# One more dependency on the transposes of the second expert: they are held until both tiles of a pair are normalised

## The chip, the cores and the metric

The kernel runs on one core of a Trainium2 chip. The metric is the time of one execution on the device in microseconds (us); the kernel before takes 1237.52 us, the median of three runs. TensorE is written PE (its weight loads, which overlap with matmuls, PEld), VectorE DVE, ScalarE ACT, GpSimd POOL, and SyncE, which issues the transfers, SP.

## What is computed

An attention without softmax is followed by two expert layers. The change lies in the second expert alone:

```python
h = x @ w_in                                   # 4608 x 512 times 512 x 1024
h_max = np.max(h, axis=-1, keepdims=True)
e = np.exp(h - h_max)
sm = e / (np.sum(e, axis=-1, keepdims=True) + 1e-09)
solu = h * sm
mu = np.mean(solu, axis=-1, keepdims=True)
var = np.mean((solu - mu) ** 2, axis=-1, keepdims=True)
ln = (solu - mu) / np.sqrt(var + 1e-06) * g_ln
return (ln @ w_out).astype(np.float32)         # times 1024 x 512
```

## The kernel before

The 4608 tokens are 36 tiles of 128, and the second expert takes them two at a time: 18 pairs, numbered 0 to 17, each with a tile 0 and a tile 1. Every product is one level of Strassen (seven block products in place of eight), and every block product is made in three passes (`mm3`, lines 191 to 196): high part times high part on L192, high times the low part of the right side on L193, and the low part of the left side times high on L194. So a matmul's line tells which pass it is, not which product.

A pair goes through three functions.

- `second(u)` makes h: seven products of two steps with three passes each, 42 matmuls with 512 columns. Their names in the trace are `ps<-rxa,rwi` and `ps<-rxb,rwi`. DVE and ACT empty the banks (L1135, L1142, L1149), which gives two tiles of 128 x 1024 for the softmax and the normalisation (`soft`); the last step of that, a `tensor_scalar` on DVE (L1188), ends for one tile after the other.
- `second_out(u)`, first half: 16 transposes on PE (L1200), four for each half q of each tile n, every four into one bank of PSUM. They are four tasks, added in the order (1,0), (1,1), (0,0), (0,1) as (tile, half). Then come the Strassen sums: ACT copies block (1,0) (L1212), DVE makes four sums (L1209: S1 from (1,1), S3 and S2 from (0,0), S4 from (0,1)). Each of the seven left sides is split into a high part by ACT (L1226) and a low part, called its correction below (L1227). The blocks A11 = (0,0), A12 = (0,1) and A22 = (1,1) are corrected by DVE, the four sums by POOL, and in the last pair two of the sums by DVE as well.
- `second_out(u)`, second half: seven products in the order A11, S2, S1, A12, S3, S4, A22, of 12 matmuls with 256 columns each (84 in all), named `ps<-rg,rwo`, `ps<-e2r,e2r` and `ps<-ws,e2r`. DVE (L1248) and ACT (L1252) empty the banks, and SP sends the rows out (L1274).

The four transpose banks and the three banks of the seven products come from one ring of four banks; for the last two pairs the transposes take theirs from the ring that `second` uses.

The order on each engine is not written by hand. Every piece of work is a task with an engine, a planned duration, the keys that it reads and writes, and a wished time `at`; `Flow.run` plays the tasks through once while the kernel is built, and whenever an engine is free in that play it takes, among the tasks that can start, the one with the smallest `at`, and among equals the one that was added first. The instructions are issued in that order. On the chip each engine keeps to it and waits where a result is not there yet. The wished times of the work around the change are: transposes and sums of pair u 17.03 us after the pair's start, `second` of the next pair 20.75 us after it, and the products of the second half 28.08 us after it.

Of the kernel before, what the change touches and what calls it, by code (L numbers as in the profile page):

```python
# [79 lines left out]
class Flow:  # L80
# [36 lines left out]
    def add(self, eng, dur, fn, r=(), w=(), at=0.0, ps=False):  # L117
        t = Task()
        t.eng, t.dur, t.fn, t.at = eng, dur, fn, at
        t.port = eng in ("POOL", "DVE") and not ps  # L120
        t.deps, t.next, t.end, t.left, t.seq = set(), [], None, 0, len(self.tasks)
        for k in {*r, *(self.pool_of[k] for k in (*r, *w) if k in self.pool_of)}:
            if k in self.writer:
                t.deps.add(self.writer[k])
            self.readers.setdefault(k, []).append(t)
        for k in w:
            t.deps.update(self.readers.get(k, ()))
            if k in self.writer:
                t.deps.add(self.writer[k])
            self.writer[k], self.readers[k] = t, []  # L130
        t.deps.discard(t)
        self.tasks.append(t)
# [48 lines left out]
def tile_kernel(ctx, tc, qkv, tail, g2, w1, w2, gl, out):  # L181
    nc = tc.nc
    PE, ACT, DVE, POOL, SP = nc.tensor, nc.scalar, nc.vector, nc.gpsimd, nc.sync
    flow = Flow()
    add = flow.add
# [930 lines left out]
    def h_name(u):  # L1116

        return "h3" if u == NU - 1 else "h2"
# [73 lines left out]
    def second_out(u, at, early=0.0):  # L1192

        bks, banks = {}, hbank if u >= NU - 2 else accs
        for n, q in ((1, 0), (1, 1), (0, 0), (0, 1)):
            bk = bks[n, q] = banks()

            def turn(n=n, q=q, bk=bk):
                for c in range(4):
                    PE.transpose(buf[bk][:, c * P:(c + 1) * P], buf[h_name(u), n][:, (4 * q + c) * P:(4 * q + c + 1) * P],  # L1200
                                 buf["ident"])

            add("PE", 0.44, turn, r=[(h_name(u), n), "ident"], w=[bk], at=at)

        def a(n, q):
            return buf[bks[n, q]].rearrange("p (c t) -> p c t", t=P)
# [10 lines left out]
        for o in (A11, S2, S1, A12, S3, S4, A22):  # L1217
# [3 lines left out]
            else:  # L1221
# [7 lines left out]
                r=[*keys, ("xth", o)], w=[("xtl", o)], at=at, ps=o in (A11, A12, A22))  # L1229
# [42 lines left out]
        for n in range(2):  # L1272
            t, k = 2 * u + n, rows[n]
            add("SP", 0.73, lambda t=t, k=k: SP.dma_start(out=out[t * P:(t + 1) * P, :], in_=buf[k]),  # L1274
                r=[k, ("out half", k, 0), ("out half", k, 1)], w=[("out", t)], at=at)
# [42 lines left out]
    def t_step(i):  # L1318
        return T0 + STEP_A * i
# [5 lines left out]
    for i, (n, c) in enumerate(order):  # L1325
        at = t_step(c + 2 * n) - CV_AHEAD
# [115 lines left out]
    for i in range(NSTEP):  # L1442
        m, c = divmod(i, CPP)
        at, d = t_step(i), STEP_A
# [31 lines left out]
    at = T1_  # L1476
# [17 lines left out]
    for n, item in enumerate([*items, None]):  # L1494
        at = item["at"] if item else T_E2
# [16 lines left out]
        else:  # L1512
# [6 lines left out]
            for b in (B11, T2, T1, B21, T3, B22, T4):  # L1519
                for kk in range(2):  # L1520
                    for part in range(2):
# [3 lines left out]
                            r=[("bd", kk, 0, b), ("bd", kk, 1, b)] + ([("b", b)] if part or kk else []), w=[("b", b)],  # L1525
                            at=at)
# [34 lines left out]
    for i in range(2 * NOP):  # L1561
        o, part = divmod(i, 2)
        if i < 8:
# [3 lines left out]
            r=[("lwd", c, o) for c in range(NC // 2)], w=[("lw", o, part)], at=T_E2 + i)  # L1567
    for u in range(NU):
        at = T_E2 + E2_AT + PAIR_C * u
        last = u == NU - 1  # L1570
        if u:
            prep_second(u, at - E2_LEAD - (LAST_PREP if last else 0))
        if last:
            rooms = [(n, i) for n in ("sf", "xf") for i in range(2)]
            flow.change(lambda: None, (*rooms, *((("xf", i), n) for i in range(2) for n in range(2))),
                        [(n, i) for n in ("h3", "e3") for i in range(2)])
            for i in range(2):
                buf["h3", i], buf["e3", i] = (buf[n, i].rearrange("p a b -> p (a b)") for n in ("sf", "xf"))
        second(u, at - (LAST_LEAD if last else 0))
        if u < NU - 2:  # L1580
            second_out(u, at + TR_LAG)
        elif last:

            second_out(u - 1, at - PAIR_C + TR_LAG - LAST_TR, LAST_TR)
            second_out(u, at - LAST_LEAD + TR_LAG - LAST_TR1, LAST_TR1)
# [51 lines left out]
```

## Time and profile before

| | |
|---|---|
| three runs, median (lowest to highest) | 1237.52 us (1237.31 to 1237.98) |
| profiled execution, its own time | 1238.22 us |
| span of that execution, first to last instruction | 1236.4 us |
| second expert, from its first transposes to the end of the span | 861.8 to 1236.4 us |
| PE busy, share of the span | 99% |
| DVE, POOL, ACT busy, share of the span | 78%, 65%, 61% |

The own time of the profiled execution is 1.8 us longer than its span, and 0.70 us longer than the median of the three runs. Matmuls are pipelined: the next one starts before the shown end of the last, so the time that a stretch of PE takes is read from start to start, not from durations.

### The profile page before, as it was taken

Reading aid. Unit: us, or ns where it says so; the run is one execution under the profiler, and the core shown is the slowest. Engines: PE = TensorE matmul, PEld = TensorE weight load, DVE = VectorE, ACT = ScalarE, POOL = GpSimd, SP = SyncE. Lnnn points to the kernel's source line nnn. Section 1 sums busy time; section 2 is a strip of 40 time slices with the busy share of each in tenths; the row PEclk is TensorE's granted clock in tenths of the full one; section 3 lists DMA queues with packets and bytes.
Section 4 is the critical chain, followed back from the end, with each engine's and each line's share of the span. In section 5 each row is a group of like instructions: output and inputs, shape, how many; then the busy total and the mean of one; then the engine's idle time right before and its main releaser. Section 6 shows DMA issues by size and latency. Waiting matters only on the chain. (4 is left out here: it accounts for less than half of the span.)

```text
span 1236.4 us, 20838 instructions
## 1 busy us (share of the span) xinstructions
PE 1222.6 (99%) x7218; PEld 1075.0 (87%) x7218; DVE 968.8 (78%) x1580; ACT 748.1 (61%) x1406; POOL 799.8 (65%) x745
## 2 busy tenths in 40 slices
PE   8999999999999999999999999999999999999998
PEld 6788888889999999888888888888999999898988
DVE  7978777787877677768787858887979787777785
ACT  5767666676663563655465636554666666666663
POOL 2367556778676647558777736476897676856622
PEclk9999999999999999999999999999999999999999
DMA  9899999689959849674977498599321111111001
GB/s 332 294 331 340 335 306 320 213 270 322 320 175 301 278 147 303 211 244 145 316 240 244 138 279 310 161 307 313 101 77 36 60 44 60 36 47 57 18 18 52
DMA packets 208265, 250.42 MB, mean 203 GB/s; under 512 B 13344, under 2 KB 140320, under 8 KB 208160
## 3 DMA queue, kind: packets, MB, share of 16 engines
q1 hardware_dynamic: 208160, 249.09, 61.3%
q8 instruction: 57, 0.93, 0.3%
q14 instruction: 48, 0.39, 0.1%
HBM read 169.87 MB, written 79.17 MB: 201 GB/s over the span
## 5 line engine op out<-in xcount | busy, mean ns | idle before, releaser
L192 PE MATMUL ps<-rg,rwo 128*128 128x512 f32 (+2 forms) x868 | 299.5, 345 | 0.6 <-DMA rwo<-wod 0.6
L194 PE MATMUL ps<-rg,rwo 128*128 128x512 f32 (+2 forms) x868 | 297.5, 343 | 0.3 <-DVE rwo L1227 0.2
L193 PE MATMUL ps<-rg,rwo 128*128 128x512 f32 (+2 forms) x868 | 297.1, 342 | 0.4 <-DVE rg L806 0.4
L192 PEld LDWEIGHTS ps<-rg,rwo 128*128 128x128 f32 x868 | 164.2, 189 | 16.7 <-DMA rwo<-wod 0.9
L193 PEld LDWEIGHTS ps<-rg,rwo 128*128 128x128 f32 x868 | 164.2, 189 | 16.4 <-DVE rg L806 0.7
L194 PEld LDWEIGHTS ps<-rg,rwo 128*128 128x128 f32 x868 | 164.1, 189 | 16.2 <-DVE rwo L1227 0.9
L809 POOL TENSOR_TENSOR rg<-fh,rg 128x384 fp32r<-128x384 f32 (+1 forms) x96 | 118.6, 1252 | 72.7 <-ACT rg L804 70.5
L192 PE MATMUL ps<-rxa,rwi 128*128 128x512 f32 (+1 forms) x384 | 146.8, 382 | 0.6 <-DVE fh L1135 0.4
L193 PE MATMUL ps<-rxa,rwi 128*128 128x512 f32 (+1 forms) x384 | 144.6, 376 | 0.0
L194 PE MATMUL ps<-rxa,rwi 128*128 128x512 f32 (+1 forms) x384 | 144.5, 376 | 0.0
L444 POOL TENSOR_TENSOR ws<-fconv,ws 128x512 fp32r<-128x512 f32 (+1 forms) x86 | 104.9, 1228 | 50.0 <-ACT ws L443 34.8
L796 ACT ACTIVATE fh<-fh,const 128x512 f32<-128x512 f32 (+1 forms) x156 | 104.7, 689 | 34.3 <-DVE fh L793 33.5
L791 ACT ACTIVATE fh<-ps 128x512 int32<-128x512 f32 (+1 forms) x126 | 71.2, 568 | 84.1 <-PE ps L194 64.8
L192 PE MATMUL ps<-rxb,rwi 128*128 128x512 f32 (+1 forms) x288 | 110.5, 384 | 0.0
L793 DVE SCALAR_TENSOR_TENSOR fh<-ps,fh 128x512 f32<-128x512 f32 (+1 forms) x126 | 80.9, 648 | 36.0 <-ACT fh L791 34.4
L193 PE MATMUL ps<-rxb,rwi 128*128 128x512 f32 (+1 forms) x288 | 108.5, 377 | 0.0
L194 PE MATMUL ps<-rxb,rwi 128*128 128x512 f32 (+1 forms) x288 | 108.4, 376 | 0.0
L426 POOL TENSOR_TENSOR fconv<-fconv 128x512 f32<-128x512 f32 x40 | 53.5, 1337 | 53.4 <-DVE fconv L424 53.4
L192 PEld LDWEIGHTS ps<-rxa,rwi 128*128 128x128 f32 x384 | 72.2, 188 | 13.4 <-DVE fh L1135 1.6
L194 PEld LDWEIGHTS ps<-rxa,rwi 128*128 128x128 f32 x384 | 72.1, 188 | 11.4
L193 PEld LDWEIGHTS ps<-rxa,rwi 128*128 128x128 f32 x384 | 72.2, 188 | 10.0
L1227 POOL TENSOR_TENSOR rwo<-fconv,rwo 128x512 fp32r<-128x512 f32 x35 | 45.3, 1298 | 53.1 <-ACT rwo L1226 52.8
(191 smaller groups left out, 3106.5 us busy)
## 6 DMA issues: line engine op xcount, KB each, us to landing
rwi<-wid SPq DMA_DIRECT2D x66, 512.0 KB, 5.7
rwo<-wod SPq DMA_DIRECT2D x80, 256.0 KB, 4.4
att<-qkv SPq DMA_DIRECT2D x32, 512.0 KB, 6.4
fconv<-w SPq DMA_DIRECT2D x28, 512.0 KB, 5.2
px<-fh SPq DMA_DIRECT2D x42, 256.0 KB, 4.2
xd<-xf SPq DMA_DIRECT2D x18, 512.0 KB, 5.7
wid<-ws SPq DMA_DIRECT2D x18, 512.0 KB, 4.0
xf<-xd SPq DMA_DIRECT2D x18, 512.0 KB, 5.6
```

What stands on the lines that cost most here:

```text
L192: PE.matmul(ps, lhsT=lh, rhs=rh, start=start, stop=False, skip_group_check=more)
L193: PE.matmul(ps, lhsT=lh, rhs=rl, start=False, stop=False, skip_group_check=more)
L194: PE.matmul(ps, lhsT=ll, rhs=rh, start=False, stop=stop, skip_group_check=more)
L426: either(on_dve, 512, lambda eng: eng.tensor_tensor(out=buf[wk], in0=buf[yk], in1=buf[wk], op=ALU.add), r=[yk, wk], w=[wk], at=at)
L444: either(on_dve, n, lambda eng: eng.tensor_tensor(out=lo(), in0=src(), in1=f(hi()), op=ALU.subtract), [*keys, *hk], lk, at)
L791: add("ACT", e_(0.6, 0.385, n), lambda: ACT.activation(out=tt().bitcast(I32), in_=h(), func=AF.Copy, scale=INV_2PI, bias=0.25), r=r, w=[tk ...
L793: add("DVE", e_(0.69, 0.418, n), lambda: DVE.scalar_tensor_tensor(out=tt(), in0=h(), scalar=INV_2PI, in1=tt().bitcast(I32), op0=ALU.mult, ...
L796: add("ACT", e_(0.725, 0.509, n), lambda: ACT.activation(out=tt(), in_=tt(), func=AF.Sin, bias=buf["halfpi"][:, 0:1], scale=TWO_PI), r=[tk ...
L809: either(on_dve, n, lambda eng: eng.tensor_tensor(out=lo(), in0=g(), in1=f(hi()), op=ALU.subtract), [*gk, *hk], lk, t + 2)
L1227: add(eng, dur, lambda o=o, src=src, eng=eng: (DVE if eng == "DVE" else POOL).tensor_tensor(out=xt(o, 1), in0=src(), in1=f(xt(o, 0)), op=A ...
```

## The change

Each of the four transpose tasks read the tile that it transposes. Now each reads both tiles of its pair, so that none can be placed before both are normalised. The work itself is the same.

```diff
             def turn(n=n, q=q, bk=bk):
                 for c in range(4):
                     PE.transpose(buf[bk][:, c * P:(c + 1) * P], buf[h_name(u), n][:, (4 * q + c) * P:(4 * q + c + 1) * P],
                                  buf["ident"])
 
-            add("PE", 0.44, turn, r=[(h_name(u), n), "ident"], w=[bk], at=at)
+            add("PE", 0.44, turn, r=[(h_name(u), 0), (h_name(u), 1), "ident"], w=[bk], at=at)
```

## Rows read from the trace of the kernel before

**Rows 1.** The page: busy time, share of the span, instructions.

```profile
PE 1222.6 (99%) x7218; PEld 1075.0 (87%) x7218; DVE 968.8 (78%) x1580; ACT 748.1 (61%) x1406; POOL 799.8 (65%) x745
```

**Rows 2.** Stretches: length, busy time of five engines, granted clock, DMA.

```profile
861.80:1202.10 340.30, 339.67 (x2221) 308.33 (x2222) 275.80 (x466) 218.62 (x417) 234.13 (x217) 1.00 0.16 52
962.87:964.54 1.67, 1.67 (x18) 1.67 (x16) 1.61 (x3) 1.03 (x3) 0.00 (x0) 1.00 0.62 187
964.54:968.75 4.21, 4.21 (x22) 3.47 (x21) 3.96 (x7) 3.64 (x8) 2.02 (x2) 1.00 0.01 1
```

**Rows 3.** Timeline of PE: rows of transposes and the second matmul behind.

```profile
962.87 1.91 PE L1200 MATMUL ps<-const,fconv 128*128 128x128 f32 x16
...
964.85 0.39 PE L193 MATMUL ps<-rxa,rwi 128*128 128x512 f32 x1
...
1025.82 1.03 PE L1200 MATMUL ps<-const,fconv 128*128 128x128 f32 x8
...
1026.92 0.40 PE L193 MATMUL ps<-rxb,rwi 128*128 128x512 f32 x1
...
1046.73 0.60 PE L1200 MATMUL ps<-const,fconv 128*128 128x128 f32 x4
...
1047.40 0.40 PE L193 MATMUL ps<-rxb,rwi 128*128 128x512 f32 x1
...
1047.87 1.47 PE L1200 MATMUL ps<-const,fconv 128*128 128x128 f32 x12
```

**Rows 4.** DVE, ACT and PE timelines around pair 7's transposes.

```profile
1004.02 0.81 DVE L1188 TENSOR_SCALAR fconv<-fconv,const 128x1024 f32<-128x1024 f32 x1
1005.43 1.29 DVE L1227 TENSOR_TENSOR rwo<-ps,rwo 128x512 fp32r<-128x512 f32 x2 [0.61 <-ACT rwo L1226]
...
1004.81 1.08 ACT L1226 CAST rwo<-ps 128x512 fp32r<-128x512 f32 x2 [2.19 <-PE ps L1200]
...
1005.75 1.04 PE L1200 MATMUL ps<-const,fconv 128*128 128x128 f32 x8
```

**Rows 5.** PE timeline: where the work of a pair begins anew.

```profile
1003.48 0.40 PE L192 MATMUL ps<-rxb,rwi 128*128 128x512 f32 x1
...
1025.12 0.40 PE L192 MATMUL ps<-rxb,rwi 128*128 128x512 f32 x1
...
1068.50 0.60 PE L1200 MATMUL ps<-const,fconv 128*128 128x128 f32 x4
...
1112.01 0.60 PE L1200 MATMUL ps<-const,fconv 128*128 128x128 f32 x4
...
1133.65 0.60 PE L1200 MATMUL ps<-const,fconv 128*128 128x128 f32 x4
...
1155.45 0.60 PE L1200 MATMUL ps<-const,fconv 128*128 128x128 f32 x4
```

**Rows 6.** DVE and PE timelines of pair 9, first product of its second half.

```profile
1052.33 0.68 DVE L1227 TENSOR_TENSOR rwo<-ps,rwo 128x512 fp32r<-128x512 f32 x1
...
1053.06 0.39 PE L194 MATMUL ps<-rg,rwo 128*128 128x256 f32 x1
```

**Rows 7.** PE timeline of pair 0, behind its second row of transposes.

```profile
864.09 1.04 PE L1200 MATMUL ps<-const,fconv 128*128 128x128 f32 x8
...
865.66 0.28 PE L192 MATMUL ps<-rg,rwo 128*128 128x256 f32 x1
```

**Rows 8.** DVE and PE timelines of the last two pairs.

```profile
1201.86 0.80 DVE L1188 TENSOR_SCALAR fconv<-fconv,const 128x1024 f32<-128x1024 f32 x1
...
1217.48 1.28 DVE L1227 TENSOR_TENSOR rwo<-ps,rwo 128x512 fp32r<-128x512 f32 x2
...
1222.15 0.68 DVE L1227 TENSOR_TENSOR rwo<-fconv,rwo 128x512 fp32r<-128x512 f32 x1
...
1202.12 1.91 PE L1200 MATMUL ps<-const,fconv 128*128 128x128 f32 x16
...
1223.81 0.28 PE L192 MATMUL ps<-rg,rwo 128*128 128x256 f32 x1
```

## The prediction

> **What bounds the kernel now.** The page comes first: PE is busy for 99% of the span, no other engine for more than 78% [rows 1]. Since the change touches one stage only, the next view is the busy time by stretches, for the stage from the first transposes of pair 0 to the last ones of pair 15: of 340.30 us PE is busy for 339.67 at a granted clock of 1.00 [rows 2]. The reader is to see that 0.63 us of visible idle time is all that a better order could win there; whatever else the change brings has to come out of the cost of the instructions themselves. The third view is PE in order of time, which shows how the transposes stand now; [rows 3] have one row of each length, the counts are read along the whole stage. Eleven of the 18 pairs have them as two rows of eight with a product step of three matmuls or more between, two (5 and 16) as one row of 16, three (9, 12, 13) as a row of four and one of twelve, and two (10 and 14) as three rows. The fourth view is DVE and ACT around them. In pair 7 the second tile is normalised from 1004.02 to 1004.83; ACT casts two blocks into `rwo` at 1004.81, which can only be A11 and A12, both of tile 0, and DVE corrects them at 1005.43, in time in which it would idle; the second row of transposes, tile 1, starts at 1005.75 [rows 4]. So tile 0 is done first, and its two corrections lie ahead of the four sums.
>
> **The change part by part.** No instruction is added or removed. Three things move.
>
> *Fewer rows.* What does starting a row of transposes cost? Take the time from the first transpose of a row to the second matmul behind the row, and take off one regular step of 0.23 us for that matmul (1047.40 to 1047.87 is two of them): 1047.40 − 1046.73 − 0.23 = 0.44 for four, 1026.92 − 1025.82 − 0.23 = 0.87 for eight, 964.85 − 962.87 − 0.23 = 1.75 for 16 [rows 3]. That is 0.109 us for each transpose and nothing for a row: two rows of eight take 1.74, one of 16 takes 1.75. The first matmul behind a row does show a longer step, 0.31 in place of 0.23 (it starts at 964.54, where the stretch of the row ends [rows 2], and the next at 964.85), but the last transpose gives the 0.08 back, since its step is shorter. I take 0 for this part. The bound on the side of a gain is that the 0.08 is real after all: 36 rows become 18, so 18 × 0.08 = 1.4 us; with the 0.63 us of idle time [rows 2], 2.0 us.
>
> A long row could also cost clock. The row of 16 in pair 5 ran 1.67 us with nothing but transposes, and the granted clock was 1.00 in it and in the 4.21 us behind it, which is the level of 2.4 GHz [rows 2]. The Trainium skill says otherwise: TensorE: Matmul & The Clock Gate, Part 4: PE-mode transpose, states that transposes do not count as a busy PE for the clock gate, so a longer block of them would work against the full clock. By the rows the sum has nothing here; by that rule each pair would pay in the matmuls behind its row, which is the third rival.
>
> *Tile 0's transposes later.* The four tasks become ready at one moment, when the second tile is normalised, with equal wished times; among equals the one added first goes first, so the row runs tile 1, then tile 0. Tile 1 hardly moves: its row starts at the first boundary between product steps after the second normalisation, as now. PE fills the place of the first row with steps of the next pair's `second`, which are ready anyway (three matmuls stand between the rows). Tile 0 comes 0.87 us behind tile 1 where it was ahead of it. The sums hardly move, since they start from tile 1's copy. What moves is the two corrections of A11 and A12, 1.28 to 1.29 us of DVE: they fall behind the sums, which were added earlier, and A11 is the first product of the second half. They also delay the DVE work queued behind the sums, L1135, which empties the banks of the next pair's `second`.
>
> The trace has this case already: in pair 9 A11 is corrected at 1052.33, only after the sums, and the low pass of the first product waits for it until 1053.06 [rows 6]. Its price is read from the length of such a pair, from one beginning of a pair's work to the next. Pair 7, in two rows of eight, takes 1025.12 − 1003.48 = 21.64. Pair 9 takes 1068.50 − 1046.73 = 21.77, pair 12 takes 1133.65 − 1112.01 = 21.64, pair 13 takes 1155.45 − 1133.65 = 21.80 [rows 3, 5]. So a late A11 costs 0.00 to 0.16, mean 0.10 us. Eight pairs (4, 6, 7, 8, 10, 11, 14, 15) go over to it: 8 × 0.10 = 0.8 us, between 0 and 1.3. Pairs 9, 12 and 13 are there already, and pair 5 keeps its row.
>
> Pairs 0 to 3 are tighter. In pair 0 the product of A11 serves as filler, 1.57 us after the second row began (864.09 to 865.66) [rows 7]; with a correction behind the sums it can't start that early: in pair 9 the correction ends at 1053.01, 5.1 us after the row of twelve began [rows 3, 6]. So 12 matmuls with 256 columns, some 1.44 us (a pair's 21.64 less 42 × 0.23 for `second` and 1.75 for the transposes leaves 10.2, or 0.12 for each of the 84), are missing as filler in each of four pairs, 5.8 us in all if nothing takes their place. Something should: the corrections that now stand ahead of L1135 are gone from there, so the banks of `second` come free earlier by up to 1.28. I take the 0.10 of pair 9 for each, 0.4 us, and keep 0 and 5.8.
>
> *The last two pairs.* In pair 16 the row of 16 starts at 1202.12, but its second tile is normalised from 1201.86 to 1202.66 [rows 8]: the row moves by 0.54. Products of pair 15 cover PE meanwhile, but the first product of pair 16 comes later by part of that: 0.2, between 0 and 0.54. In pair 17 the corrections of A11 and A12 (1.28 us at 1217.48) lie between the two rows now; behind the sums they push the correction of S2, which DVE makes there at 1222.15 to 1222.83 and which PE uses from 1223.81 [rows 8]. The slack is 0.98, so 1.28 − 0.98 = 0.3 us, between 0 and 1.28. Nothing is behind these to hide them; PE runs without a gap to the end from there.
>
> *The sum.* 0 + 0.8 + 0.4 + 0.2 + 0.3 = 1.7 us. The profiled execution took 1238.22, so 1239.9 by its own time. It lies 0.70 above the median of the runs shown, so the forecast for the median is 1237.52 + 1.7 = 1239.2 us. About 0.2% of it, 2.5 us, is what a measurement of this kernel can tell from no change; 1.7 us is 0.14%.
>
> **The rivals.**
>
> *Starved filler, slower.* The place is pairs 0 to 3: PE has no A11 to fall back on while it waits for the banks of `second`, and nothing comes in its place. For it speaks that the filler is used there, at 865.66 [rows 7]; against it, that the later pairs with a late A11 lose at most 0.16. Full price 5.8 in place of 0.4, so 1.7 + 5.4 = 7.1 and 1244.6 us; at half the price, 1241.7. It decides from 1.2 us on in these four pairs, since the other terms make 1.3 and the bound is 2.5.
>
> *A row costs something, faster.* If the 0.08 at each row were saved, and the visible idle time with it, 2.0 us would go: 1235.5. The three row lengths lie on one line through nothing [rows 3], and even this stays just inside 2.5 us; it takes a better order of the whole tail of the stage as well.
>
> *The clock falls.* If the 4.21 us behind each row of 16 ran at half the clock they would take twice as long: 16 pairs without a row of 16 now, 16 × 4.2 = 67 us, some 1305. The clock of 1.00 in pair 5 speaks against it [rows 2].
>
> *The rows don't form.* The banks of (0,0) and (0,1) are the ones that the pair before used last; where they come free after the normalisation, or the play finds a task of smaller wished time between, the row stays split and nothing moves: 1237.5. The order of the tasks in pairs 5 and 16 speaks against it.
>
> **How the numbers follow.** The forecast has a chance of 0.48, rows that don't form or a shift that costs nothing 0.10; both lie within 0.2%. Starved filler (or a larger price of the late A11) from 2.5 us on has 0.37, the gain from rows 0.04, the clock 0.01. So slower 0.38, same 0.58, faster 0.04. The range goes down to 1236.3, which leaves the larger gains out, and up to 1243.3, four fifths of the full price of the starved filler; about one in ten is left out on either side. The forecast's own range is 1237.5 to 1240.0.
>
> **What the profile after would show.** Rows of 16 on L1200 in nearly every pair, each taking 1.67 us to the next matmul at a clock of 1.00. ACT's copy L1212 ahead of the casts into `rwo` in each pair. DVE's corrections of A11 and A12 behind the sums. The third pass of the first `rg,rwo` matmuls waiting some 0.1 to 0.2 us for L1227. Idle time of PE in the stage of 1 to 3 us in place of 0.63. The prediction is wrong if PE idles for whole product steps in pairs 0 to 3, if the order of tile 1 and tile 0 stays as it is, or if a row of 16 takes less than 1.6 us.

## Result

The changed kernel takes 1255.46 us (median of four runs, 1254.69 to 1257.27), the kernel before 1237.48 in the same comparison: ratio 1.0144, 95% interval 1.0132 to 1.0156, so 18.0 us slower. The forecast was 1239.2 with a range to 1243.3.

**The profile after.** PE's busy time rose by 3.4 us and its share of a span of 1252.9 us fell to 98% (set it beside [rows 1]). The page's first line, then stretches of PE work (set them beside [rows 2]; columns as there):

```profile
PE 1226.0 (98%) x7218; PEld 1077.3 (86%) x7218; DVE 960.9 (77%) x1580; ACT 747.9 (60%) x1406; POOL 787.9 (63%) x745
```

```profile
860.00:952.00 92.00, 82.91 (x535) 75.47 (x535) 66.31 (x115) 54.66 (x105) 61.52 (x61) 0.96 0.24 75
952.00:1192.00 240.00, 236.48 (x1552) 214.85 (x1551) 181.89 (x317) 149.11 (x286) 153.44 (x150) 1.00 0.14 45
...
863.52:865.19 1.67, 1.67 (x17) 1.66 (x15) 0.41 (x1) 0.74 (x2) 0.00 (x0) 1.00 1.02 324
...
868.38:870.69 2.31, 2.31 (x11) 2.31 (x12) 2.31 (x4) 0.98 (x3) 2.31 (x3) 0.50 1.13 325
870.69:872.58 1.89, 1.89 (x8) 1.52 (x8) 1.25 (x2) 0.82 (x2) 1.02 (x2) 0.72 0.30 79
...
939.64:942.91 3.27, 3.27 (x16) 3.27 (x17) 3.17 (x5) 1.58 (x4) 3.05 (x3) 0.56 0.00 0
942.91:944.54 1.63, 1.63 (x7) 1.32 (x7) 0.39 (x1) 0.03 (x1) 0.00 (x0) 0.84 0.00 0
```

The reader is to see three things. In the first 92 us of the stage, pairs 0 to 3, PE idles for 9.1 us (92.00 less 82.91). The row of 16 itself ran at a clock of 1.00 and took 1.67 us, as pair 5's did before. And at two places in that stretch the granted clock falls to half: summed over the last four stretches shown, length times the missing share of the clock is 2.31 × 0.50 + 1.89 × 0.28 + 3.27 × 0.44 + 1.63 × 0.16 = 3.4 us.

**Where the time went.** The start of the seventh product (A22, from `ws`) is a landmark in every pair; what PE has done of the next pair's `second` by then differs somewhat between kernels, so a single landmark can be off by a few steps. PE timeline, pairs 3, 14 and 17, first of the kernel before, then of the changed one:

```profile
939.37 0.28 PE L192 MATMUL ps<-ws,e2r 128*128 128x256 f32 x1
...
1175.62 0.28 PE L192 MATMUL ps<-ws,e2r 128*128 128x256 f32 x1
...
1231.01 0.28 PE L192 MATMUL ps<-ws,e2r 128*128 128x256 f32 x1
```

```profile
951.01 0.28 PE L192 MATMUL ps<-ws,e2r 128*128 128x256 f32 x1
...
1191.87 0.28 PE L192 MATMUL ps<-ws,e2r 128*128 128x256 f32 x1
...
1247.70 0.28 PE L192 MATMUL ps<-ws,e2r 128*128 128x256 f32 x1
```

So 11.6 us are lost by pair 3, 4.6 more by pair 14 (16.25), and 0.4 in the last three pairs (16.69). These are the two profiled executions, whose spans differ by 16.5 us (1252.9 less 1236.4); the medians differ by 18.0. In pair 0, PE, DVE and ACT in order of time in the changed kernel:

```profile
862.03 0.50 PE L192 MATMUL ps<-rxb,rwi 128*128 128x512 f32 x1 [0.68 <-ACT fh L1142]
...
863.52 1.91 PE L1200 MATMUL ps<-const,fconv 128*128 128x128 f32 x16
865.67 0.38 PE L192 MATMUL ps<-rg,rwo 128*128 128x256 f32 x1 [0.24 <-ACT rwo L1226]
865.89 0.28 PE L193 MATMUL ps<-rg,rwo 128*128 128x256 f32 x1
868.38 0.58 PE L194 MATMUL ps<-rg,rwo 128*128 128x256 f32 x1 [2.21 <-DVE rwo L1227]
```

```profile
864.78 0.69 DVE L1209 TENSOR_TENSOR fconv<-ps,fconv 128x512 f32<-128x512 f32 x1 [1.66 <-ACT fconv L1212]
...
867.65 1.28 DVE L1227 TENSOR_TENSOR rwo<-ps,rwo 128x512 fp32r<-128x512 f32 x2
868.85 0.68 DVE L1135 TENSOR_TENSOR fconv<-ps,fh 128x512 f32<-128x512 f32 x1
```

```profile
864.16 0.59 ACT L1212 COPY fconv<-ps 128x512 f32<-128x512 f32 x1 [2.18 <-PE ps L1200]
865.03 0.59 ACT L1226 CAST rwo<-ps 128x512 fp32r<-128x512 f32 x1 [0.29 <-PE ps L1200]
...
868.77 0.59 ACT L1149 COPY fconv<-ps 128x512 f32<-128x512 f32 x1
```

The same work in pair 0 of the kernel before, DVE and ACT:

```profile
863.18 1.28 DVE L1227 TENSOR_TENSOR rwo<-ps,rwo 128x512 fp32r<-128x512 f32 x2
864.38 1.47 DVE L1135 TENSOR_TENSOR fconv<-ps,fh 128x512 f32<-128x512 f32 x2
865.83 1.42 DVE L1209 TENSOR_TENSOR fconv<-ps,fconv 128x512 f32<-128x512 f32 x2
...
863.42 0.61 ACT L1149 COPY fconv<-ps 128x512 f32<-128x512 f32 x1
```

Tile 1's copy (L1212) is now ahead of the cast of A11. DVE, which corrected A11 and A12 from 863.18 on in the kernel before, idles for 1.66 us, makes the four sums, and corrects A11 from 867.65. In PE's order the first product of the second half comes right behind the row (865.67, as in [rows 7]), and PE stands in its third pass until 868.38. Nor could a step of `second` have filled the place: the next one in PE's order needs a bank that L1149 or L1135 empties, and these start at 868.77 and 868.85 only, where they started at 863.42 and 864.38 before. Pairs 1, 2 and 3 repeat it with waits of 1.75, 1.80 and 2.42 us, and in each of them, too, L1149 starts behind the end of the stand, by 0.15 us. With 0.68 and 0.24 us in pair 0 these waits are the 9.1 us. In later pairs the wait is another one. Pair 8, PE and DVE:

```profile
1047.65 0.28 PE L194 MATMUL ps<-rg,rwo 128*128 128x256 f32 x1
1048.23 0.50 PE L192 MATMUL ps<-rxa,rwi 128*128 128x512 f32 x1 [0.30 <-DVE fh L1135]
```

```profile
1045.70 1.28 DVE L1227 TENSOR_TENSOR rwo<-ps,rwo 128x512 fp32r<-128x512 f32 x2
1046.90 0.68 DVE L1227 TENSOR_TENSOR e2r<-ps,e2r 128x512 fp32r<-128x512 f32 x1
1047.50 1.47 DVE L1135 TENSOR_TENSOR fh<-ps,fh 128x512 f32<-128x512 f32 x2
```

The bank that the next pair's product needs is emptied behind the corrections. The step of 0.58 us (1047.65 to 1048.23) where 0.12 is regular is 0.46 lost, though the profile calls only 0.30 of it a wait: it draws a matmul of 256 columns 0.28 us long, 0.16 more than its step, and counts from that end. Pairs 4 to 14 each show such a gap, of 0.43 to 0.51.

### The profile page after: what moved, and what is told of

Read it like the earlier page. It is cut to its first block, busy times and chain, and to the rows that moved or that the text cites. A ratio compares the mean times of both kernels' runs of the same rounds, so it can differ in the third digit from the quotient of the medians.

```text
span 1252.9 us, 20859 instructions
## 1 busy us (share of the span) xinstructions
PE 1226.0 (98%) x7218; PEld 1077.3 (86%) x7218; DVE 960.9 (77%) x1580; ACT 747.9 (60%) x1406; POOL 787.9 (63%) x745
## 4 chain that ended last, share of the span: by engine, by line
PE 86%; DVE 8%; ACT 2%; DMA 2%; issue 1%; POOL 1%; SPq 0%; DVEq 0%; ACTq 0%; POOLq 0%
PE ps L192 27%; PE ps L194 27%; PE ps L193 27%; DVE fconv L1209 3%; PE ps L662 2%; DMA att<-qkv 2%; DVE rwo L1227 1%; PE ps L544 1%; PE ps L694 1%; PE ps L1200 1%; ACT e2r L1226 1%; DMA rwo<-wod 1%; DVE e2r L1227 1%; ACT fconv L1212 1%; DVE fh L1135 0%
## 5 line engine op out<-in xcount | busy, mean ns | idle before, releaser
L194 PEld LDWEIGHTS ps<-rxa,rwi 128*128 128x128 f32 x384 | 72.1, 188 | 11.4
L732 POOL TENSOR_TENSOR sf<-xf 128x256 f32<-128x256 f32 x72 | 63.0, 875 | 25.2 <-DMA xf<-px 15.7
```

Source lines behind the costliest of these rows:

```text
L194: PE.matmul(ps, lhsT=ll, rhs=rh, start=False, stop=stop, skip_group_check=more)
L732: add("POOL", 0.74, lambda: POOL.tensor_tensor(out=out_(), in0=in0(), in1=in1(), op=fn), r=[*keys, *r], w=w, at=at)
```

## Experiments

All are compared with the kernel before, which took 1237.6 to 1237.9 us beside them.

**tile0_first.** The change, with the four tasks in another order on the same banks:

```diff
-        for n, q in ((1, 0), (1, 1), (0, 0), (0, 1)):
-            bk = bks[n, q] = banks()
...
+        bks = {nq: banks() for nq in ((1, 0), (1, 1), (0, 0), (0, 1))}
+        for n, q in ((0, 0), (0, 1), (1, 0), (1, 1)):
+            bk = bks[n, q]
```

> All four transpose tasks still wait for both tiles, but they are added in the order (0,0), (0,1), (1,0), (1,1), on the banks that they have in the changed kernel, so that the row of 16 runs tile 0 first. Order theory (the 18 us come from the corrections of A11 and A12 falling behind the sums, because tile 1 is transposed first): DVE makes them ahead of the sums again, and the time comes back to 1237 to 1242 us, with less than 2 us of PE waits on L1227. Wait theory (the wait for both tiles itself costs, whatever the order inside the row): 1252 to 1256 us.

Measured 1240.93 us, ratio 1.0026 (1.0017 to 1.0036). The wait for both tiles stays, and 14.5 of the 18 us are gone. Its busy time from pair 4 on, then PE's waits from 850 on (waiting instruction, what it waited for: us in total, times, longest):

```profile
940.00:1200.00 260.00, 260.00 (x1707) 237.32 (x1706) 208.28 (x357) 160.31 (x312) 155.09 (x156) 1.00 0.14 45
```

```profile
PE ps L192 <- ACT fh L1142: 2.0, 3, 0.7
PE ps L194 <- DVE rwo L1228: 1.4, 1, 1.4
```

No wait is shown between 940 and 1200. What remains are three waits for L1142 in the first pairs, whose place the first row of eight used to fill, and some at the end, the longest of 1.4 us in pair 16 (the correction's line is L1228 here).

**late_corr.** The kernel before, with only the corrections of A11 and A12 held back:

```diff
-                r=[*keys, ("xth", o)], w=[("xtl", o)], ...
+                r=[*keys, ("xth", o), *([("sum", S4)] if o in (A11, A12) else [])], w=[("xtl", o)], ...
```

> The kernel before, its transposes as they were, with one thing added: the corrections of A11 and A12 on DVE may only come after the sum S4. Order theory: this alone brings most of the loss, 1249 to 1257 us, with PE waiting on L1227 in the first pairs. Wait theory: the transposes are not held up, so 1236 to 1240 us.

Measured 1243.03 us, 1.0042 (1.0027 to 1.0057): 5.4 us, between the two expectations. Late corrections cost without any change to the transposes. The largest wait, of 2.5 us, is in pair 0, and the clock fell behind it (last section):

```profile
PE ps L194 <- DVE rwo L1227: 4.1, 3, 2.5
```

**pairs_4_17, pairs_0_3.** The change in a part of the pairs, `u >= 4` or `u < 4`:

```diff
-            add("PE", 0.44, turn, r=[(h_name(u), n), "ident"], w=[bk], at=at)
+            add("PE", 0.44, turn, r=[*((h_name(u), i) for i in range(2) if i == n or u >= 4), "ident"], w=[bk], at=at)
```

> The change in pairs 4 to 17 alone. If pairs 0 to 3 carry most of the loss (order theory: there A11 is needed soonest; the trace shows waits of 1.9 to 2.6 us in each of the four, and the clock at half behind two of them), 1242 to 1246 us remain. If the loss is the same in every pair, 14 of 18 parts of it remain: 1251 to 1252 us.

> The change in pairs 0 to 3 alone. The change in pairs 4 to 17 alone cost 4.1 us of the 18; if the two parts add, 1237.6 + 13.9, so 1250 to 1253 us. If the loss of pairs 4 to 17 only shows behind the disturbed first pairs, or the other way round, it lies outside of that.

Measured 1241.69 us, 1.0033 (1.0020 to 1.0046), and 1249.28 us, 1.0092 (1.0077 to 1.0107). Pairs 0 to 3 cost 11.4 us, pairs 4 to 17 4.1; both lie just below what was expected, and together they leave some 2.5 us of the 18. Part of that is clock: the four runs of the change have a mean granted clock of 0.9963, those of pairs_0_3 0.9975, and over 1250 us the difference is an estimated 1.6 us. PE's largest wait in each, pairs_4_17 first:

```profile
PE ps L192 <- DVE fh L1135: 2.6, 9, 0.3
```

```profile
PE ps L194 <- DVE rwo L1227: 8.2, 4, 2.4
```

**tile0_0_3.** Pairs 0 to 3 wait for both tiles, tile 0 first in the row; the rest as before (tile0_first under `if u < 4`).

> Pairs 0 to 3 hold all transposes until both tiles are normalised, but tile 0 goes first in the row; pairs 4 to 17 are as before. By the beginnings of the last product, the trace of tile0_first is 5.0 us behind the kernel before in pair 3 and the changed kernel 11.6, so if the wait alone costs in the first pairs what the order doesn't, 1241 to 1244 us. If the order is all of it: 1237 to 1239 us.

Measured 1239.19 us, 1.0013 (1.0004 to 1.0023): 1.3 us, just above the "order is all of it" expectation. In the same four pairs the change costs 11.4 with tile 1 first and 1.3 with tile 0 first. The three waits for L1142 are most of its visible loss:

```profile
PE ps L192 <- ACT fh L1142: 2.0, 3, 0.7
```

**corr_first.** The changed kernel; casts and corrections of A11 and A12 (the loop's body, now the function `left`) are added ahead of the sums:

```diff
+        for o in (A11, A12):
+            left(o)
         add("ACT", 0.59, lambda: ACT.copy(out=total(S3), in_=a(1, 0)), ...
...
-        for o in (A11, S2, S1, A12, S3, S4, A22):
+        for o in (S2, S1, S3, S4, A22):
```

> The changed kernel with its row of 16, tile 1 first, but the casts and corrections of A11 and A12 are added ahead of the sums, so that DVE and ACT prefer them. Order theory, if the late A11 is what PE starves on: 1238 to 1244 us. If it is the late emptying of the banks of second (L1135 stands behind the same amount of DVE work here): 1248 to 1256 us.

Measured 1247.91 us, 1.0082 (1.0067 to 1.0097). Preferring the corrections takes back 7.5 of the 18 us, between the two expectations: with tile 1 transposed first they still come late. In pair 0 the row starts at 865.50, the cast of A11 at 867.01, and its correction at 868.23, behind two of the sums.

**banks_first.** The changed kernel; L1135 and L1149 are wished for 8 us earlier (`at=at - 8`).

> The changed kernel, but DVE's L1135 and ACT's L1149 are wished for 8 us earlier, so that they go ahead of the sums and corrections as soon as h2 is free. Bank theory (PE starves because the banks of second are emptied late): 1240 to 1249 us although the correction of A11 comes later still. A11 theory (PE starves because the first product of the second half is not ready): 1255 us or more.

Measured 1251.08 us, 1.0108 (1.0093 to 1.0123): 4.4 us back, also between the two. With steps of `second` to run in the meantime PE waits for the corrections 1.3 us in all, in place of 8.8 in the changed kernel, though they come later still; so the late banks are a part of the cause. How large a part this run can't say, since h2 still comes free only behind the whole row: the waits moved to L1135. The changed kernel, then this one:

```profile
PE ps L194 <- DVE rwo L1227: 8.8, 6, 2.4
...
PE ps L192 <- DVE fconv L1135: 5.4, 8, 1.2
PE ps L194 <- DVE rwo L1227: 1.3, 2, 0.9
```

**release_both, release_and_late.** Pairs 0 to 16 share one pair of buffers for h, called h2, so the transposes also decide when the next pair may write its h. In the kernel before, one more key (`tok`), which L1149 writes and the last three L1135 read, holds that back until all four tasks are done; the second kernel adds late_corr to it.

```diff
-        add("ACT", 0.59, lambda: ACT.copy(out=place(), in_=buf[bA]), r=[bA], w=keys, at=at)
+        add("ACT", 0.59, lambda: ACT.copy(out=place(), in_=buf[bA]), r=[bA], w=[*keys, *tok], at=at)
...
-            add("PE", 0.44, turn, r=[(h_name(u), n), "ident"], w=[bk], at=at)
+            add("PE", 0.44, turn, r=[(h_name(u), n), "ident", *(["tok"] if u < NU - 2 else [])], w=[bk], at=at)
```

> The kernel before, its transposes in the old order with their old dependencies. Added: the next pair's second may write its h (L1149 and the three L1135 that write h2) only when all four transpose tasks of the pair are done, through one more key; the two tiles of h2 are one buffer for all pairs but the last, so until now tile 0's part was free after tile 0's transposes. Release theory (the change costs because it keeps h2 of tile 0 and so the banks of second): a good part of the loss comes with this alone, 1241 to 1250 us. Theory that only the late correction of A11 counts: 1237 to 1239 us.

> The kernel before with both side effects of the change and without the change: h2 is released after all four transpose tasks, and the corrections of A11 and A12 come after the sum S4. If these two together are the cause: 1249 to 1258 us, more than the two single losses added (5.4 us for the late corrections alone). If the row of 16 or the wait for both tiles has a cost of its own that is missing here: 1243 to 1247 us.

Measured 1241.40 us, 1.0029 (1.0018 to 1.0040), and 1244.96 us, 1.0063 (1.0048 to 1.0078). Keeping h2 costs 3.7 us by itself, late corrections 5.4, both together 7.3. I had expected more than the two added; it is less, in the range that I gave for a cost of the row or the wait itself. tile0_first has both of these and loses 3.3 us only, so they don't hold the 10.7 us that are missing. What these kernels still lack of the change is that tile 1 is transposed and copied first; here tile 0 is.

**hybrid, order_only, order_all.** hybrid is tile0_first in pairs 4 to 15 and the kernel before elsewhere. order_only has the new order in those pairs and no wait for both tiles; order_all has it in all 18.

> Pairs 4 to 15 hold all transposes until both tiles are normalised, tile 0 first in the row; pairs 0 to 3, 16 and 17 are as before. In tile0_first PE was busy for all of the 260 us from 940 to 1200, and its losses lie in pairs 0 to 3 and in the last two. If they stay away here: 1236.5 to 1238.5 us, the same as the kernel before. If the row costs something in every pair: 1239 to 1241 us.

> The kernel before with the four transpose tasks of pairs 4 to 15 added tile 0 first, on their old banks, and no wait for both tiles. It is hybrid without the wait. If hybrid's gain of 2.6 us comes from holding the transposes until both tiles are normalised (one row of 16 behind which the sums, the corrections and the banks of second fall in a better order): 1237 to 1239 us. If it comes from the order in which the tasks are added: 1234.5 to 1236 us.

> As order_only, but with tile 0 added first in all 18 pairs, and no wait for both tiles. If the order in which the tasks are added helps wherever both tiles are ready at about one moment: 1233 to 1236 us, no worse than order_only (1235.4). If it hurts in the last two pairs, where tile0_first lost about 2.8 us in PE waits of the two: 1236 to 1239 us.

Measured 1235.02 us, 0.9979 (0.9969 to 0.9988); 1235.43 us, 0.9981 (0.9972 to 0.9991); 1235.39 us, 0.9982 (0.9972 to 0.9991). All three beat the kernel before by 2.4 to 2.6 us, hybrid against both its expectations, and no part of the wait in that can be told from these runs: the order in which the tasks are added is enough, as the second expectation for order_only had it, and it needs no more than the pairs 4 to 15. The landmarks of pairs 3, 8 and 14 in order_only, then that of pair 8 in the kernel before:

```profile
938.59 0.28 PE L192 MATMUL ps<-ws,e2r 128*128 128x256 f32 x1
...
1044.49 0.28 PE L192 MATMUL ps<-ws,e2r 128*128 128x256 f32 x1
...
1172.86 0.28 PE L192 MATMUL ps<-ws,e2r 128*128 128x256 f32 x1
```

```profile
1045.29 0.28 PE L192 MATMUL ps<-ws,e2r 128*128 128x256 f32 x1
```

These eleven pairs take 234.27 us in place of 236.25, and the gain lies in the last six: pair 3 is ahead by 0.78 us (from work that is the same in both), pair 8 by 0.80, pair 14 by 2.76.

## Why the prediction was wrong

- *Fewer rows, 0 us.* Right as far as the runs show. A row of 16 takes 1.67 us to the next matmul, and no gain from having fewer is seen.
- *Clock.* Right for the row, which ran at 1.00. Not foreseen: behind PE's stands in pairs 0 and 3 the clock fell, 3.4 us in all in the profiled execution.
- *Tile 0 second in the row, its corrections behind the sums, the sums hardly moved.* The mechanism was right, and it is the cause: in pairs 0 to 3, 11.4 us with tile 1 first against 1.3 with tile 0 first; in pairs 4 to 15 no wait of PE is shown with tile 0 first. The sums even came sooner in pair 0 (864.78 in place of 865.83).
- *Pairs 0 to 3, 0.4 us with a bound of 5.8.* This is the step that failed. It took the price of pair 9, and as upper end the 1.44 us of missing filler in each pair. Neither bounds what happened. With neither A11 nor an emptied bank of `second`, PE stands until the correction lands, whatever the length of the filler was: three waits of 1.75 to 2.42 us and one of 2.21 make 8.2 us, and the clock comes on top. Measured 11.4 to 11.6. The starved-filler rival named the place and the mechanism; its full price of 7.1 us for the whole change was less than half of the 18. The prediction's own first sign of being wrong, PE idle for whole product steps in pairs 0 to 3, is what came.
- *"Something should" take the filler's place, since L1135's banks come free earlier.* Wrong, and the other half of the same step. They came free later. In pair 0 the first L1135 that writes h2 moved from 864.38 to 868.85 and L1149 from 863.42 to 868.77, because the write needs tile 0's transposes to have read h2, and by then the sums and corrections, with their smaller wished times, stood ahead. I had not listed that h2 is released by the transposes; alone, this costs 3.7 us, and emptying the banks sooner in the changed kernel takes 4.4 back.
- *Pairs 4 to 15, 0.8 us.* Too small: 4.6 us by the landmarks for pairs 4 to 14, 4.1 for pairs 4 to 17 run alone. Pairs 9, 12 and 13 were no model: in 9 and 13 one of the two corrections was still made early, and in 12, the one with no price at all, both were (1114.40 is the second, below). With both behind the sums, L1135 comes later and PE loses some 0.46 us at it in each pair. Nor did pair 5 "keep its row": before, its row ran tile 0 first, with both corrections ahead of the sums, so it changed like the others (sums at 977.56, corrections at 980.35 afterwards). Pairs 5 and 12 in the kernel before:

```profile
964.13 1.29 DVE L1227 TENSOR_TENSOR rwo<-ps,rwo 128x512 fp32r<-128x512 f32 x2
965.60 1.42 DVE L1209 TENSOR_TENSOR fconv<-ps,fconv 128x512 f32<-128x512 f32 x2 [0.18 <-ACT e2r L1226]
...
1114.40 0.69 DVE L1227 TENSOR_TENSOR rwo<-ps,rwo 128x512 fp32r<-128x512 f32 x1 [0.44 <-ACT rwo L1226]
1115.38 1.42 DVE L1209 TENSOR_TENSOR fconv<-ps,fconv 128x512 f32<-128x512 f32 x2 [0.29 <-ACT e2r L1226]
```

- *The last two pairs, 0.5 us.* The sum is about right, 0.4 over the last three pairs, partly by luck: pair 17 has two new waits for L1227, of 0.21 and 0.36 us, and one of 0.20 us that pair 16 had before is gone.
- *0.63 us of visible idle time as all that a better order can win.* Wrong as well: order_only wins 2.4 us, 2.0 of it in pairs 4 to 14, where the visible idle time falls only from 0.63 to 0.34 us (the lengths less PE's busy time, below). As in pair 8 above, the view counts as a wait only part of what the starts show.

```profile
939.37:1175.62 236.25, 235.62 (x1552) 214.10 (x1551) 186.57 (x322) 151.96 (x288) 163.37 (x151) 1.00 0.14 47
...
938.59:1172.86 234.27, 233.93 (x1553) 214.01 (x1551) 186.24 (x323) 150.27 (x289) 163.36 (x151) 1.00 0.14 47
```

What stays open: how the loss in pairs 0 to 3 divides between late corrections, late release of h2 and late casts. Single side effects cost 3.7 and 5.4 us, preferring single consumers takes back 7.5 and 4.4, and they don't add. Why order_only gains in pairs 9 to 14 and not in 4 to 8 was not followed up.

## What to carry to other kernels

A dependency that only "waits a little for its twin" also changes who goes first among equals, and releases whatever buffer the task reads: list both before pricing the wait. Where an engine's next product needs one late operand, and what could fill its place is held up as well, price the whole stand up to that operand, not the length of the work that was the filler. Before holding work together, try the order alone: here it won 2.4 us without the wait, and with the wait it decided between a loss of 18 us (tile 1 first) and one of 3.3 (tile 0 first).

## What the runs showed of the hardware

In the changed kernel the granted clock fell to 0.50, the level of 1.2 GHz, behind PE's stands in pairs 0 and 3 (2.49 us from the start of one matmul at 865.89 to the next at 868.38, and 2.71 from 936.93 to 939.64). Behind the stands of pairs 1 and 2 it stayed at 1.00; PE's starts are 2.03 and 2.09 us apart there (889.92 to 891.95, 914.75 to 916.84), and the stretches behind are:

```profile
891.95:895.40 3.45, 3.45 (x22) 3.19 (x23) 3.35 (x5) 2.13 (x6) 3.45 (x4) 1.00 0.00 0
916.84:920.00 3.16, 3.16 (x21) 2.96 (x22) 3.06 (x5) 1.62 (x4) 3.16 (x4) 1.00 0.00 0
```

The same stand need not do the same again. pairs_0_3 runs pair 0 in the same order, with the row of 16 right ahead of the product of A11 and the same stand of 2.49 us (865.11 to 867.60), and there the clock stayed at 1.00; in late_corr it fell behind a stand of 2.76 us (866.93 to 869.69) that has no row of 16 near it (two rows of eight, six matmuls of 512 columns behind the second). The stretches behind the two stands, pairs_0_3 first, then late_corr:

```profile
867.60:872.00 4.40, 4.40 (x31) 4.14 (x32) 4.26 (x7) 2.00 (x4) 2.85 (x3) 1.00 1.04 318
...
871.10:874.40 3.30, 3.30 (x13) 2.82 (x12) 2.81 (x4) 0.95 (x4) 3.16 (x3) 0.50 0.30 77
```

In tile0_first it fell (0.51 from 1213.80 to 1217.30) behind shorter stands, 1.69 us from 1210.11 to 1211.80 and 0.77 from 1212.97 to 1213.74. So the length of the stand alone does not decide, and a kernel whose PE stands pays for the clock in some executions and not in others: of the four runs of the change the longest, 1257.27 us, has the lowest mean clock, 0.995. The Trainium skill, TensorE: Matmul & The Clock Gate, Part 4: PE-mode transpose, says that transposes do not count as a busy PE in the same way. The rows of 16 alone were not seen to lower the clock (1.00 in [rows 2] and in 863.52 to 865.19 above); whether a row adds to the stand behind it, as that rule would have it, these runs don't show: late_corr needed none, and in pairs_0_3 the row and the stand of pair 0 together lowered nothing.
